# A new order around the two forms of seven products, second-weight sums on GpSimd, later stores of first weights

## The chip, the cores and the metric

The kernel runs on one core of one Trainium2 chip. The metric is the device time of one execution in microseconds (us); the median of three runs of the kernel before is 1193.54 us, from 1193.38 to 1194.54.

## The reference

Three stages in a row, on 2304 tokens of 512 features: attention over a small memory, a dense layer with a leaky activation, and four experts whose outputs are added with weights from normalized probabilities. The change touches the experts alone.

```python
def _moe2_ref(x, domain_probs, w1, w2):
    p = domain_probs / (domain_probs.sum(-1, keepdims=True) + 1e-09)
    out = np.zeros((N, D), dtype=np.float32)
    for e in range(E):                      # E = 4, D = 512, F = 1024
        h = np.maximum(x @ w1[e], 0.0)
        out += p[:, e:e + 1] * (h @ w2[e])
    return out.astype(np.float32)
```

## The kernel before

All products are made in a high and a low part: an operand is cast on ScalarE (the high part, `hi`) and the rest is subtracted on VectorE or GpSimd (the low part, `lo`), and three products of 128 x 288 stand for one (`PASSES`). What follows calls six or twelve such matmuls that stand together a block or a product.

The experts are done in *units*. A unit is 512 hidden features (`g`, 0 to 7) for 576 tokens (`b`, 0 to 3). The first half of the units (`half` 0) does b = 0 and 1 for all g, the second half b = 2 and 3; within a pair of units t = 0 and t = 1 stand for the two b. So there are 32 units, the first from 404 us on, the second half from about 790 us on.

Each unit makes the first product of the experts (class `Up`, twice: hp = 0 and 1) with seven block products p1 to p7 in place of eight. They are formed in three banks of PSUM, x, y and w: p1 and p2 into x; p6, p7 and p4 into y; p5 and p3 into w. Between them intermediate states are read: `v1` (ScalarE, of x after p1), `v16` (VectorE, y after p6, plus v1), `v167` (VectorE, y after p7, plus v1). p2 can start only when v1 has been read, p7 after v16, p4 after v167. `c11`, `c22`, `c21` and `c12` write the four blocks of the hidden layer, which is then gated (`gate`, `gate_half`: the maximum with 0 times the probability, on VectorE).

Between these blocks stand the *side products*, the second product of the experts for the unit before (`down()`, `old.product(n)`), each followed by a *flush* on VectorE or ScalarE that adds it to an accumulator. Their results take turns in two PSUM banks, so product n+2 waits for flush n. In most of the second half (`Seven`) the second product too has a form of seven, P1 to P7, two side products of six matmuls each (n = 0 to 13). Its operands are differences of blocks (`sum`, on VectorE, in place), cast (`hi`, ScalarE) and given a low part (`lo`, on GpSimd or VectorE). In the other units it has eight side products of twelve matmuls (`Down`). At the end `combine` adds the seven accumulators of b = 2 and 3 into four (seven sums each on VectorE).

The second weights have, for the form of seven, four sums S1, S2, S4, S3 (`s_sum`) whose parts (`s_part`) are made in the first half of the units and stored to memory; so are the parts of the first weights (`w1_lo`, `keep`, 1792 KB a store). Two S tiles and four part tiles are reused in turn, so a later cast waits for an earlier store.

There is no scheduler: each engine works its own queue in the order in which the code in `run_experts` issues. `extra(place)` issues what the table `more[(hp, place)]` holds: place 0 comes after v16, 1 after c11, 2 after c22, 3 after the gate, 4 after c12. Every transfer is issued on SyncE's queue (SP).

## Time and profile before

| | before |
|---|---|
| median of three runs | 1193.54 us |
| the profiled execution's own time | 1192.46 us |
| its span | 1190.7 us |
| TensorE busy (PE) | 1144.2 us, 96% |
| VectorE busy (DVE) | 871.6 us, 73% |
| ScalarE busy (ACT) | 472.8 us, 40% |
| GpSimd busy (POOL) | 378.3 us, 32% |
| experts, from the start | about 404 to 1188 us |

The profiled execution is one run beside the three; its span is what the trace covers. TensorE is nearly always busy, so its gaps are what to look for.

### The profile page before, as it was taken

How to read it: one execution, taken by the hardware profiler on the slowest of the kernel's cores; microseconds unless marked ns; L12 is line 12 of the kernel's file. 1: busy time of each engine (PE TensorE's matmuls, PEld its weight loads, DVE VectorE, ACT ScalarE, POOL GpSimd, SP SyncE). 2: the span in 40 equal slices, each digit the busy share in tenths (PEclk: the TensorE clock that was granted, in tenths of full speed). 3: DMA queues.
4: the chain of work that ended last, by engine and by line, in shares of the span. 5: the costliest groups of instructions: out<-in, count | busy, mean ns of one | idle time of the engine just before them, and what ended most of it. 6: DMA issues, size and time to landing. Idle time of an engine off the chain costs nothing.

```text
span 1190.7 us, 21752 instructions
## 1 busy us (share of the span) xinstructions
PE 1144.2 (96%) x8628; PEld 1093.4 (92%) x8628; DVE 871.6 (73%) x1601; ACT 472.8 (40%) x1035; POOL 378.3 (32%) x305
## 2 busy tenths in 40 slices
PE   8799999999999989999999999999999999999988
PEld 6578999999999989999999999899999999999988
DVE  6999888885567666666776676686577777777784
ACT  5567665554455534242232323233422222222220
POOL 2332023221010252554434535432323332333230
PEclk9999999999999999999999999999999999999999
DMA  9641221301000455464654554674555455545512
GB/s 377 258 173 28 63 90 53 107 20 79 1 1 1 179 199 222 169 228 187 221 211 175 195 228 178 208 269 163 179 173 164 151 170 150 164 151 187 158 48 71
DMA packets 64214, 180.02 MB, mean 151 GB/s; under 512 B 6640, under 2 KB 23024, under 8 KB 60400
## 3 DMA queue, kind: packets, MB, share of 16 engines
q1 hardware_dynamic: 64112, 178.63, 43.4%
q8 instruction: 68, 1.11, 0.4%
q14 instruction: 34, 0.28, 0.1%
HBM read 114.34 MB, written 64.26 MB: 150 GB/s over the span
## 4 chain that ended last, share of the span: by engine, by line
PE 71%; issue 13%; DVE 8%; POOL 4%; DMA 2%; ACT 2%; SPq 0%; DVEq 0%; ACTq 0%; POOLq 0%
PE o L908 16%; PE y L600 16%; PE h L562 8%; PE uy L802 8%; PE c L972 7%; PE ux L802 6%; PE uw L802 6%; POOL gc L232 3%; PE pw L523 2%; DMA kS<-S 1%; DVE S L232 1%; DMA rawin<-in_w_in 1%; DVE xt L664 1%; DVE g L232 1%; PE pm L325 0%
## 5 line engine op out<-in xcount | busy, mean ns | idle before, releaser
L908 PE MATMUL o<-g,w 128*128 128x288 f32 x1536 | 224.7, 295 | 0.9 <-DVE acc L925 0.9
L908 PEld LDWEIGHTS o<-g,w 128*128 128x128 f32 x1536 | 210.4, 188 | 1.6 <-DVE acc L925 1.3
L600 PE MATMUL y<-g,wout 128*128 128x288 f32 x1440 | 205.6, 297 | 0.0
L600 PEld LDWEIGHTS y<-g,wout 128*128 128x128 f32 x1440 | 194.2, 188 | 10.5 <-issue 7.0
L802 PE MATMUL uy<-x,w 128*128 128x288 f32 x1152 | 186.9, 297 | 13.9 <-DVE v L836 13.9
L802 PEld LDWEIGHTS uy<-x,w 128*128 128x128 f32 x1152 | 163.3, 189 | 18.4 <-DVE v L836 18.4
L972 PE MATMUL c<-gc,w2c 128*128 128x288 f32 x1008 | 164.3, 296 | 7.4 <-POOL gc L232 5.3
L972 PEld LDWEIGHTS c<-gc,w2c 128*128 128x128 f32 x1008 | 142.8, 188 | 10.9 <-POOL gc L232 8.5
L232 POOL TENSOR_TENSOR gc<-h,gc 128x576 fp32r<-128x576 f32 x56 | 88.3, 1597 | 169.2 <-issue 123.7
L802 PE MATMUL ux<-x,w 128*128 128x288 f32 x768 | 123.7, 296 | 5.6 <-ACT v L840 5.6
L232 POOL TENSOR_TENSOR w<-raww,w 128x512 fp32r<-128x512 f32 (+1 forms) x48 | 80.4, 1689 | 142.6 <-ACT w L507 82.4
L802 PE MATMUL uw<-x,w 128*128 128x288 f32 x768 | 122.5, 295 | 0.0
L802 PEld LDWEIGHTS ux<-x,w 128*128 128x128 f32 x768 | 109.3, 189 | 6.5 <-ACT v L840 6.5
L562 PE MATMUL h<-a,wp 128*128 128x288 f32 x720 | 108.8, 296 | 0.1
L802 PEld LDWEIGHTS uw<-x,w 128*128 128x128 f32 x768 | 108.8, 188 | 0.0
L925 DVE TENSOR_TENSOR acc<-o,acc 128x288 f32<-128x288 f32 x112 | 50.9, 454 | 75.0 <-PE o L908 75.0
L562 PEld LDWEIGHTS h<-a,wp 128*128 128x128 f32 x720 | 99.5, 188 | 2.7 <-issue 1.3
L581 DVE SCALAR_TENSOR_TENSOR pos<-neg,nal,pos 128x288 f32<-128x288 f32 x120 | 64.8, 545 | 43.0 <-ACT pos L576 42.5
L959 ACT CAST gc<-h 128x576 fp32r<-128x576 f32 x70 | 47.3, 676 | 119.0 <-DVE h L951 78.2
L836 DVE TENSOR_TENSOR v<-uy,v 128x288 f32<-128x288 f32 x128 | 58.0, 453 | 42.9 <-PE uy L802 41.9
L575 ACT ACTIVATE neg<-h 128x288 f32<-128x288 f32 x128 | 53.0, 414 | 83.7 <-PE h L562 78.6
L987 DVE TENSOR_TENSOR acc<-c,acc 128x288 f32<-128x288 f32 x96 | 43.6, 455 | 52.5 <-PE c L972 50.2
(163 smaller groups left out, 1624.3 us busy)
## 6 DMA issues: line engine op xcount, KB each, us to landing
kw<-w SPq DMA_DIRECT2D x16, 1792.0 KB, 7.1
raww<-in_w SPq DMA_DIRECT2D x32, 512.0 KB, 3.7
w<-kw SPq DMA_DIRECT2D x32, 512.0 KB, 4.7
kS<-S SPq DMA_DIRECT2D x56, 256.0 KB, 2.9
w2c<-kS SPq DMA_DIRECT2D x28, 512.0 KB, 3.6
kw<-w SPq DMA_DIRECT2D x25, 512.0 KB, 2.9
w<-kw SPq DMA_DIRECT2D x48, 256.0 KB, 4.4
kv<-in_kv SPq DMA_DIRECT2D x8, 1152.0 KB, 12.4
```

Of the source, the lines that this page charges most:

```text
L232: eng.tensor_tensor(out=out, in0=in0, in1=in1.bitcast(F32), op=ALU.subtract)
L562: mm(p, wp_t[b, c, f // 2][:, x, o2 + g * 256:o2 + g * 256 + 128], a_t[b][:, y, g, o:o + HB], start=(n == 0), stop=(n == 5))
L575: nc.scalar.activation(out=neg, in_=p, func=AF.Relu, scale=-1.0)
L581: nc.vector.scalar_tensor_tensor(out=pos, in0=neg, scalar=nal[:, ft:ft + 1], in1=pos, op0=ALU.mult, op1=ALU.add)
L600: mm(First.acc[d], w[:, x, d * 128:(d + 1) * 128], self.gt[:, y, 0:HB], start=(self.start and n == 0), stop=(self.stop and n == 2))
L802: mm(p, w[:, x, a, k], operand(self.b, i)[:, y, k], start=(start and n == 0), stop=(n == 5), skip_group_check=not start)
L836: nc.vector.tensor_tensor(out=out, in0=x, in1=y, op=ALU.add)
L908: mm(self.p, w[:, x, i, d % 2 * 128:(d % 2 + 1) * 128], g, start=(m == 0), stop=(m == 11))
L925: nc.vector.tensor_tensor(out=a, in0=self.p, in1=a, op=ALU.add)
L959: nc.scalar.copy(out=t[:, 0], in_=self.raw[q])
L972: mm(self.p, w[:, x, i, m * 128:(m + 1) * 128], self.g_t[q][:, y, i], start=(k == 0), stop=(k == 5))
L987: nc.vector.tensor_tensor(out=a, in0=self.p, in1=a, op=ALU.add)
```

## The change

Three edits. In `run_experts` the side products of the form of seven and the differences, casts and low parts of their operands are issued at other places: no side product between p5 and p2, two of them between p7 and p4; the differences of P7 and P6 of the unit before come earlier, that of P4 earlier and that of P5 later. The sums S1 to S4 move from VectorE to GpSimd, and the parts of S4 and S3 from the first unit of a pair into the second. The store of the first weights of hp = 1 is issued at the end of a pair's first unit, behind the stores of S1 and S2. With the last g, five of the seven `combine` sums of b = 2 are issued in the unit's second half and two in the next unit.

```diff
--- before.py
+++ after.py
@@ -709,6 +709,10 @@
             sub_to(eng, w[:, 1], src, w[:, 0])
         raw_t.pop(("w1", 2 * g + hp))
         load_raw()
+        if hp == 0:
+            w1_keep(g, hp)
+
+    def w1_keep(g, hp):
         kept_t["w1", g, hp] = keep(w1_t[g, hp], f"kw1{g}{hp}")
 
     def keep(t, name):
@@ -743,7 +747,7 @@
         t = pools["xt"].tile([128, 2, HB], F32, tag="xt", name=f"{n}{g}").rearrange("p k n -> p (k n)")[:, 0:512]
         cs_t[g, n] = [t]
         x, y = (cs_t[g, i][0] if i in ("S1", "S2") else a[i] for i in (x, y))
-        nc.vector.tensor_tensor(out=t, in0=x, in1=y, op=op)
+        nc.gpsimd.tensor_tensor(out=t, in0=x, in1=y, op=op)
 
     def s_part(g, n, part):
 
@@ -1024,13 +1028,19 @@
                     more.setdefault((1, 1), []).extend(f + (0,) for f in w2)
                 else:
                     more.setdefault((0, 0), []).extend(f + (1,) for f in w2)
+                if t == 0:
+                    more.setdefault((1, 4), []).append((w1_keep, g, 1))
                 if g < NG - 1:
                     for place, fs in (
                         ((1, 1), [(s_sum, g, "S1"), (s_part, g, "S1", 0)]),
                         ((1, 2), [(s_part, g, "S1", 1), (s_sum, g, "S2"), (s_part, g, "S2", 0)]),
-                        ((1, 3), [(s_sum, g, "S4"), (s_part, g, "S2", 1), (s_part, g, "S4", 0)]),
-                        ((1, 4), [(s_sum, g, "S3"), (s_part, g, "S4", 1), (s_part, g, "S3", 0)]),
-                    ) if t == 0 else (((0, 1), [(s_part, g, "S3", 1)]),):
+                        ((1, 3), [(s_part, g, "S2", 1), (s_sum, g, "S4")]),
+                        ((1, 4), [(s_sum, g, "S3")]),
+                    ) if t == 0 else (
+                        ((0, 1), [(s_part, g, "S4", 0)]),
+                        ((0, 2), [(s_part, g, "S4", 1), (s_part, g, "S3", 0)]),
+                        ((0, 4), [(s_part, g, "S3", 1)]),
+                    ):
                         more.setdefault(place, []).extend(fs)
 
             loads = {}
@@ -1042,8 +1052,11 @@
                 else:
                     loads = {2 * q + 1: [(w2_load, g, q % 2, q // 2)] for q in range(4)}
             if half and g == NG - 1:
-                for n in range(7):
-                    more.setdefault(((0, 2), (0, 3), (0, 4), (1, 0), (1, 2), (1, 3), (1, 4))[n], []).append((combine, b, n))
+                places = ((1, 2), (1, 3), (1, 3), (1, 4), (1, 4)) if t == 0 else ((0, 2), (0, 3), (0, 4), (1, 0), (1, 2), (1, 3), (1, 4))
+                if t == 1:
+                    more[0, 1] = [(combine, b - 1, 5), (combine, b - 1, 6)]
+                for n, place in enumerate(places):
+                    more.setdefault(place, []).append((combine, b, n))
             if n_unit > 1:
 
                 h0, g0, b0 = units[n_unit - 1]
@@ -1117,33 +1130,34 @@
                     last.lo(0, nc.vector if hp == 0 else nc.gpsimd)
                 extra(0)
                 down(hp == 1)
-                if hp == 1 and seven:
-                    c.sum(P5)
-                    c.hi(P5)
-                u.p5()
                 if old_seven:
-                    down()
-                    if hp == 1:
+                    if hp == 0:
+                        old.sum(P7)
+                        old.hi(P7)
+                        old.lo(P7, nc.gpsimd)
+                        old.lo(P3, nc.vector)
+                    else:
                         old.sum(P4)
                         old.hi(P4)
-                        old.lo(P6, nc.gpsimd)
+                u.p5()
                 u.p2()
                 u.c11()
                 down(hp == 1)
-                if old_seven and hp == 0:
-                    old.sum(P7)
-                    old.hi(P7)
-                    old.lo(P3, nc.vector)
                 extra(1)
                 u.p7()
                 u.v167()
                 u.c22()
+                extra(2)
+                down(True)
+                down()
+                if hp == 0 and old_seven:
+                    old.sum(P6)
+                    old.hi(P6)
+                if hp == 1 and seven:
+                    c.sum(P5)
+                    c.hi(P5)
                 if hp == 1 and old_seven:
                     old.lo(P4, nc.gpsimd)
-                extra(2)
-                down(True)
-                if hp == 1 and seven:
-                    c.lo(P5, nc.vector)
                 u.p4()
                 u.c21()
                 if seven:
@@ -1151,6 +1165,8 @@
                     if hp == 0:
                         c = Seven(g, b, u)
                         c.hi(P1)
+                        if old_seven:
+                            old.lo(P6, nc.gpsimd)
                         c.lo(P1, nc.gpsimd)
                     else:
                         c.second(u)
@@ -1159,14 +1175,14 @@
                 else:
                     u.gate(1)
                     if hp == 0:
+                        if old_seven:
+                            old.lo(P6, nc.gpsimd)
                         u.hi(1)
                         u.lo(1, nc.gpsimd)
                 extra(3)
                 down(True)
-                if hp == 0 and old_seven:
-                    old.sum(P6)
-                    old.hi(P6)
-                    old.lo(P7, nc.gpsimd)
+                if hp == 1 and seven:
+                    c.lo(P5, nc.vector)
                 u.p3()
                 u.c12()
                 extra(4)
```

How it moves instructions is seen at three places. The first is TensorE's queue in a unit of seven, here the one of g = 4 and b = 3 (it starts at 1003.1 us in the trace before), hp = 0. `uw430`, `ux430`, `uy430` are the banks w, x, y; `c420` to `c425` are the side products 0 to 5 of the unit before. Before:

```order
L802 MATMUL uy430_11879<-x31_9560,w170_8821 128x288 x6
L972 MATMUL c421_11892<-gc0_9598,w2c40_11642 128x288 x6
L802 MATMUL uw430_11900<-x31_9560,w170_8821 128x288 x6
L972 MATMUL c422_11907<-gc1_9751,w2c41_11675 128x288 x6
L802 MATMUL ux430_11864<-x33_9603,w170_8821 128x288 x6
L972 MATMUL c423_11923<-gc1_9751,w2c41_11675 128x288 x6
L802 MATMUL uy430_11879<-x33_9603,w170_8821 128x288 x6
L972 MATMUL c424_11945<-gc2_9867,w2c42_11715 128x288 x6
L802 MATMUL uy430_11879<-x35_9605,w170_8821 128x288 x6
L972 MATMUL c425_11965<-gc2_9867,w2c42_11715 128x288 x6
```

And with the change:

```order
L806 MATMUL uy430_11879<-x31_9560,w170_8821 128x288 x6
L976 MATMUL c421_11892<-gc0_9598,w2c40_11642 128x288 x6
L806 MATMUL uw430_11904<-x31_9560,w170_8821 128x288 x6
L806 MATMUL ux430_11864<-x33_9603,w170_8821 128x288 x6
L976 MATMUL c422_11919<-gc1_9750,w2c41_11688 128x288 x6
L806 MATMUL uy430_11879<-x33_9603,w170_8821 128x288 x6
L976 MATMUL c423_11938<-gc1_9750,w2c41_11688 128x288 x6
L976 MATMUL c424_11946<-gc2_9836,w2c42_11719 128x288 x6
L806 MATMUL uy430_11879<-x35_9605,w170_8821 128x288 x6
L976 MATMUL c425_11969<-gc2_9836,w2c42_11719 128x288 x6
```

The side product after p5 (`uw`) has gone behind p7 (the second row of `uy` with `x33`), so that two stand between p7 and p4 (`uy` with `x35`).

The second place is GpSimd's queue in the same unit: low parts of operands of the second product, from `h430` for P1 of this unit, from `h420` for P7, P6 and P4 of the unit before, from `c0` for P2; the last row belongs to the next unit. Before, in the order P1, P7, P6, P4, P2:

```order
L232 TENSOR_TENSOR gc0_9598<-h430_11921,gc0_9598 128x576
L232 TENSOR_TENSOR gc0_9598<-h420_11665,gc0_9598 128x576
L232 TENSOR_TENSOR gc1_9751<-h420_11665,gc1_9751 128x576
L232 TENSOR_TENSOR gc2_9867<-h420_11665,gc2_9867 128x576
L232 TENSOR_TENSOR gc2_9867<-c0_9699,gc2_9867 128x576
L232 TENSOR_TENSOR gc1_9751<-h520_12178,gc1_9751 128x576
```

And with the change, in the order P7 and P6 (one row), P1, P4, P2:

```order
L232 TENSOR_TENSOR gc0_9598<-h420_11661,gc0_9598 128x576 x2
L232 TENSOR_TENSOR gc1_9750<-h430_11917,gc1_9750 128x576
L232 TENSOR_TENSOR gc1_9750<-h420_11661,gc1_9750 128x576
L232 TENSOR_TENSOR gc2_9836<-c0_9697,gc2_9836 128x576
L232 TENSOR_TENSOR gc0_9598<-h430_11917,gc0_9598 128x576
```

P1 has moved behind P7 and P6, and P7 is the first of the unit, as the next unit's row shows too. The number of instructions is the same.

The third place is GpSimd's queue in the first pair of units (g = 0), from the gated block's low parts `g000` to those of the next unit's `g010`; `w2000` to `w2011` are low parts of the second weights. Before:

```order
L232 TENSOR_TENSOR g000_5173<-h000_5154,g000_5173 128x576 x2
L232 TENSOR_TENSOR w2000_5219<-raww20_3453,w2000_5219 128x512
L232 TENSOR_TENSOR w2010_5224<-raww21_5114,w2010_5224 128x512
L232 TENSOR_TENSOR w2001_5310<-raww20_3453,w2001_5310 128x512
L232 TENSOR_TENSOR w2011_5315<-raww21_5114,w2011_5315 128x512
L232 TENSOR_TENSOR g010_5372<-h010_5335,g010_5372 128x576
```

And with the change:

```order
L232 TENSOR_TENSOR g000_5171<-h000_5152,g000_5171 128x576 x2
L232 TENSOR_TENSOR w2000_5217<-raww20_3453,w2000_5217 128x512
L232 TENSOR_TENSOR w2010_5222<-raww21_5114,w2010_5222 128x512
L750 TENSOR_TENSOR S10_5227<-raww20_3453,raww21_5114 128x512
L750 TENSOR_TENSOR S20_5245<-S10_5227,raww20_3453 128x512
L750 TENSOR_TENSOR S40_5262<-raww21_5114,S20_5245 128x512
L750 TENSOR_TENSOR S30_5273<-raww20_3453 128x512
L232 TENSOR_TENSOR w2001_5299<-raww20_3453,w2001_5299 128x512
L232 TENSOR_TENSOR w2011_5304<-raww21_5114,w2011_5304 128x512
L232 TENSOR_TENSOR g010_5369<-h010_5324,g010_5369 128x576
```

The four sums `S10`, `S20`, `S40` and `S30` now stand between the two pairs of low parts; they were on VectorE.

## Rows read from the trace of the kernel before

**Rows 1.** The page's head: span, and busy time of each engine.

```profile
span 1190.7 us, 21752 instructions
PE 1144.2 (96%) x8628; PEld 1093.4 (92%) x8628; DVE 871.6 (73%) x1601; ACT 472.8 (40%) x1035; POOL 378.3 (32%) x305
```

**Rows 2.** Timeline of TensorE, 760 to 1150 us: start, length, instruction; brackets name waits.

```profile
828.92 0.93 PE L972 MATMUL c<-gc,w2c 128*128 128x288 f32 x5 [0.61 <-POOL gc L232]
852.18 0.92 PE L972 MATMUL c<-gc,w2c 128*128 128x288 f32 x5 [0.68 <-POOL gc L232]
869.69 1.06 PE L802 MATMUL uy<-x,w 128*128 128x288 f32 x6 [0.67 <-DVE v L836]
...
1018.09 0.93 PE L972 MATMUL c<-gc,w2c 128*128 128x288 f32 x5 [0.22 <-POOL gc L232]
...
1130.46 1.06 PE L802 MATMUL uy<-x,w 128*128 128x288 f32 x6 [0.67 <-DVE v L836]
```

**Rows 3.** Chain of waits, 905 to 1105 us: start, length, what.

```profile
909.96 10.37 issue
...
1099.64 10.37 issue
```

**Rows 4.** Timeline of one unit of seven, 1003 to 1029 us.

```profile
1004.73 0.96 PE L802 MATMUL uy<-x,w 128*128 128x288 f32 x6
1005.30 0.75 DVE L863 SCALAR_TENSOR_TENSOR c<-c,p 128x576 f32<-128x576 f32 x1
...
1009.49 0.96 PE L802 MATMUL uy<-x,w 128*128 128x288 f32 x6
...
1011.40 0.45 DVE L836 TENSOR_TENSOR v<-uy,v 128x288 f32<-128x288 f32 x1
...
1015.16 4.78 POOL L232 TENSOR_TENSOR gc<-h,gc 128x576 fp32r<-128x576 f32 x3 [10.39 <-issue]
...
1017.36 1.29 DVE L863 SCALAR_TENSOR_TENSOR h<-h,p 128x576 f32<-128x576 f32 x1
```

**Rows 5.** Timeline, 404 to 432 us, and a table by windows, whose header names its columns.

```profile
415.85 2.99 POOL L232 TENSOR_TENSOR w<-raww,w 128x512 fp32r<-128x512 f32 x2
...
418.84 0.95 PE L802 MATMUL uw<-x,w 128*128 128x288 f32 x6
...
423.65 0.62 ACT L755 CAST S<-S 128x512 fp32r<-128x512 f32 x1 [0.72 <-DMA kS<-S]
...
424.62 1.81 PE L802 MATMUL ux<-x,w 128*128 128x288 f32 x6 [4.82 <-ACT v L840]
...
429.32 0.96 PE L802 MATMUL uy<-x,w 128*128 128x288 f32 x6
...
core 0: us, PE busy (x) PEld busy (x) DVE busy (x) ACT busy (x) POOL busy (x), PEclk, DMA share, GB/s
...
424.60:429.00 4.40, 4.38 (x22) 4.38 (x23) 4.18 (x6) 2.45 (x5) 2.69 (x2) 0.64 0.76 249
```

**Rows 6.** Timeline of TensorE, 440 to 640 us: first and last of five waits.

```profile
474.54 1.06 PE L802 MATMUL ux<-x,w 128*128 128x288 f32 x6 [0.28 <-ACT v L840]
...
624.47 1.06 PE L802 MATMUL uy<-x,w 128*128 128x288 f32 x6 [0.67 <-DVE v L836]
```

**Rows 7.** Timeline of TensorE, 1122 to 1146 us.

```profile
1138.45 1.03 PE L972 MATMUL c<-gc,w2c 128*128 128x288 f32 x6 [2.15 <-DVE acc L987]
...
1143.60 0.93 PE L972 MATMUL c<-gc,w2c 128*128 128x288 f32 x5 [1.60 <-POOL gc L232]
```

**Rows 8.** Timeline of GpSimd (706 and 754 us) and of TensorE (712 us).

```profile
706.79 3.00 POOL L232 TENSOR_TENSOR w<-raww,w 128x512 fp32r<-128x512 f32 x2 [2.08 <-ACT w L507]
...
712.76 1.74 PE L908 MATMUL o<-g,w 128*128 128x288 f32 x12
...
754.46 2.55 POOL L232 TENSOR_TENSOR w<-raww,w 128x512 fp32r<-128x512 f32 x2 [2.08 <-ACT w L507]
```

## Prediction

> **What bounds the kernel now.** The page comes first: TensorE is busy for 1144.2 of 1190.7 us, VectorE for 73%, GpSimd for 32% [rows 1]. Time can be won only where TensorE stands still. The second view is therefore the timeline of TensorE alone; a bracket at a row's end names what it waited for. Of the waits between 404 us (start of the experts) and the end, the change touches three families.
>
> First, the units of seven products, from 813 us on. Twelve of them have a p4 that waits for VectorE's v167 (869.69 to 1130.46, one a unit), and each has a side product that waits for GpSimd's low half: 828.92, 852.18, then one a unit as at 1018.09 [rows 2]. Their cost is read from the chain of waits, where the same wait of GpSimd recurs every (1099.64 - 909.96) / 8 = 23.71 us, once a unit [rows 3]. A block of six matmuls takes (1009.49 - 1004.73) / 6 = 0.793 us where nothing waits [rows 4]; 28 of them are 22.2 us. So about 1.45 us a unit are lost, with a little left for the 28 starts. The two brackets say only 0.67 + 0.22 [rows 2]: a wait costs some 0.28 us more than its bracket.
>
> Second, the first half, where the sums of the second weights are made. One stall is large: p2 of the second unit stands for 4.82 us, because v1 is queued on ScalarE behind casts that wait for a store to land [rows 5]. From p5 (418.84) to p4 (429.32) lie p5, p2, p7 and a side product of two blocks, 5 x 0.793 = 3.97 us; the rows are 10.48 apart, so 6.5 us are lost. That is more than the wait: behind it TensorE's granted clock was 0.64 in the mean [rows 5], partly its level of 1.2 instead of 2.4 GHz. Five smaller waits lie between 474.54 and 624.47 (0.28, 0.65, 0.65, 0.52 and 0.67 us [rows 6]); with 0.28 each on top, 4.2 us.
>
> Third, the unit from 1122 to 1146 us: waits of 2.15 and 1.60 [rows 7].
>
> **The seven-product units.** The new order has two side products instead of one between p7 and p4, and one less between p5 and p2. v167 now ends at 1011.40 + 0.45 = 1011.85 where p4 was due at 1009.49 + 2 x 0.793 = 1011.08 [rows 4]. In the new order p7 is block 7 of the unit (from 0), ends at 8 x 0.793 = 6.35 us, v167 runs from 6.6 (TensorE's results are taken up 0.2 us after a block) to 7.05, and p4 is block 10, due at 7.9: margin 0.9. v16, which p7 needs, stays at about 3.2 against p7's 5.55.
>
> On GpSimd the low half of P7 stood second in a run of three of 1.6 each from 1015.16 [rows 4], and its product came before it was done. Now P7's sum is on VectorE at 3.8 to 4.4, its cast ends at 5.2, its low half at 6.7, and its product is block 17, due at 13.5. P6: sum 8.6 to 9.2, cast to 9.9, low half to 11.7, due at 22 x 0.793 = 17.4. P1 follows it to 13.2, due in the next unit. P4: sum from 14.9, low half to 17.9, due at 19.8. P5's slips to 22.5, due at 34 x 0.793 = 27. I can lay out no wait that is left. So 11 units give 1.45 each, 16.0; the first two, with a GpSimd wait alone, 0.61 + 0.28 and 0.68 + 0.28; the last one's p4, 0.67 + 0.28. Sum **18.7 us**.
>
> **The last units.** Five of the seven sums of b=2 go to the second half of the unit at 1122 us and two into the next. Both waits there go, 2.15 + 1.60 + 0.56 = 4.3. But at 22.3 us into that unit VectorE is behind: a gate, four sums of 0.7, three flushes and two adds after p4 keep it until about 25.2, the next gate to 25.9, v16 to 26.3, where p7 is due at 25.5; and the two sums push v167 0.7 us past p4. With restarts I give 1.9 back: **2.4 us** net, bounds 4.3 (no backlog) and 0.
>
> **The sums on GpSimd.** Seven pairs of units. The trace has no such sum on GpSimd; its nearest row is a low half of the same 128x512, two in 2.55 us alone and in 3.00 where VectorE works beside it [rows 8], so 1.28 to 1.5 each; I take 1.28. In the pair at 699 us the low halves begin at 706.79 and, with VectorE's sum gone, end at 709.3; S1 ends at 710.6, S2 at 711.9. ScalarE's cast of S1 (0.62) ends at 711.3. VectorE's low half of S1 waits for it, and behind that on VectorE stands the flush whose bank the product at 712.76 needs [rows 8].
>
> Does S2's sum hold this low half up as well? A gate on VectorE takes 0.75 us alone and 1.29 at 1017.36, inside GpSimd's run [rows 4]: an operation that reads two SBUF tiles waits for GpSimd's current one. Then the low half ends at 712.4, the flush at 712.8, and TensorE loses about 0.2 us in six of the pairs: **-1.2 us**. The Trainium skill speaks against the edit here, in "SBUF — State Buffer", section "Who interferes with whom": a VectorE instruction with two SBUF inputs and a GpSimd one that reads SBUF exclude each other, and the second fully blocks. By that rule the sum is the one below; were the engines independent, the flush would be done by 712.4 and the sum some 3 us better. The trace agrees (1.29 against 0.75).
>
> The gain there: the casts of S4 and S3 move into the next unit, when the stores of S1 and S2 have landed, and the 1.8 MB store of first weights no longer lies before those. The five small waits should go: **4.2 us**. The large one does not simply go. The first unit has no side products, so it is short. GpSimd's low halves begin at 415.85 [rows 5] and end at 418.2 to 418.4, S1 at 419.6, S2 at 420.9, and ScalarE reaches v1 only after S2's cast: 421.9, with p2 due at 419.64. VectorE is held by S1's low half until 421.4 and at two gates by S4's and S3's sums, so v16 ends near 425.8, and p7 starts there instead of at 426.22. With p4 at 428.4, if the clock does not fall behind these shorter waits, I count **0.8** of the 6.5; bounds 0 and 6.5.
>
> The later store costs nothing in my sum. Behind it on SP's queue stand the loads of the next raw weights, which GpSimd's w1 sums need 9 us later (at 724 us in that pair). Without that cover these sums slip by about 1 us, and no product waits for them at once.
>
> **Sum.** 18.7 + 2.4 - 1.2 + 4.2 + 0.8 = 24.9 us. The profiled execution took 1192.46 us (the span and 1.8 around it); that gives 1167.5. The median of the runs lies 1.1 above it, so **1168.5 us**.
>
> **Rivals.** (a) The sums on GpSimd cost more: the flush slips by one contended sum, 1.5 us instead of 0.2, in seven pairs: 25 - 7 x 1.3 = 16 us, 1177.5. For it: the flush has no margin, and ScalarE waits in order too. Against: GpSimd is busy for 32% of the span only [rows 1]. (b) The units of seven keep half of their loss, as a wait in another place (P4's low half, the densest one on GpSimd): 25 - 9 = 16, again 1177.5. Against: margins of 0.9 us and more. (c) The order brings nothing in those units, since the waits follow VectorE's total load and only move: 25 - 21 = 4, 1189.5. Against: the timeline names the same two places in every unit [rows 2]. (d) Slower: ScalarE's casts and VectorE queue behind the sums in the first half. That decides from 25 / 7 = 3.6 us lost in each pair, which two sums of 3 us instead of 1.28 would do; at 4.2 us a pair it ends near 1198. No GpSimd row of that size reaches 2 us. (e) Better: the first pair's 6.5 us go whole, no flush and no sum is late: 25 + 5.7 + 1.2 + 1.9 = 33.8, 1160.
>
> **How the numbers follow.** Forecast (1162 to 1174) 0.60, (a) 0.15, (b) 0.11, (c) 0.03, (d) 0.04, (e) 0.07. The likeliest is 1168.5. The range takes in (a) and (b) and stops short of (e): 1162 to 1180, leaving out (c), (d), (e) and tails. A difference under 0.2% (2.4 us) can't be told from none: faster 0.93, same 0.03, slower 0.04.
>
> **What would show it.** Right: the period of the units of seven falls from 23.71 to about 22.3 us, with no bracket on p4 or on P7's product; the five small waits of the first half are gone, and brackets of 0.1 to 0.2 us appear there on the last side product of a pair's first unit; p2 and p7 of the second unit still wait, with p4 near 428.5; in the last unit p7 and p4 wait for VectorE, 0.7 us each. Wrong: sums on GpSimd well over 1.3 us, casts of S1 or S2 that end after v1 was due, or TensorE waiting inside the units of seven.

## The result, and the profile after

The changed kernel takes 1174.71 us (median of four runs, 1174.5 to 1175.75), the kernel before, run beside it, 1193.9 us. The ratio is 0.984 (95% interval 0.982 to 0.986): faster, by 19 us. The prediction said 1168.5, with 1162 to 1180 as its range.

The page's head after, for [rows 1]:

```profile
span 1172.7 us, 21803 instructions
PE 1142.6 (97%) x8628; PEld 1096.0 (93%) x8628; DVE 844.3 (72%) x1573; ACT 473.0 (40%) x1035; POOL 406.7 (35%) x333
```

VectorE has 28 instructions fewer and GpSimd 28 more, the sums of seven groups. TensorE works almost as long as before; its waits have shrunk. What it waits for from the start of the experts, as total, times and longest:

```profile
PE uy L806 <- DVE v L840: 8.0, 7, 3.1
PE ux L806 <- ACT v L844: 2.2, 1, 2.2
PE o L912 <- ACT acc L927: 1.6, 1, 1.6
PE o L912 <- DVE g L232: 1.1, 2, 0.9
PE o L912 <- DVE acc L929: 0.8, 2, 0.6
PE c L976 <- ACT acc L989: 0.5, 2, 0.3
PE c L976 <- DVE acc3xt L991: 0.2, 1, 0.2
```

No line names GpSimd any more. The next view is TensorE's timeline, read by units: from a unit's first p1 to the next one's. In us, the profiled executions of before and after, and of three experiments told below:

| unit (half, g, t) | before | after | operands_moved | products_moved | sums_back |
|---|---|---|---|---|---|
| start of the experts | 404.48 | 406.18 | 404.58 | 404.37 | 405.01 |
| (0,0,1) | 30.33 | 31.90 | 31.05 | 30.69 | 27.31 |
| (0,1,0) | 24.12 | 25.71 | 24.11 | 24.12 | 24.13 |
| (0,1,1) | 25.30 | 23.83 | 25.31 | 25.31 | 23.83 |
| (0,2,0), as five of t = 0 | 23.83 | 24.10 | 23.83 | 23.83 | 23.84 |
| (0,3,1) | 24.95 | 23.83 | 24.58 | 24.56 | 23.84 |
| (0,4,1) | 25.55 | 23.84 | 25.47 | 25.56 | 23.83 |
| (1,0,1) | 23.18 | 22.79 | 22.31 | 23.13 | 22.79 |
| (1,1,0) | 23.25 | 22.82 | 22.31 | 23.21 | 22.82 |
| (1,2,0), as eleven of its kind | 23.71 | 22.28 | 22.31 | 22.92 | 22.28 |
| (1,7,0) | 27.47 | 22.67 | 24.39 | 26.42 | 22.67 |
| (1,7,1) to the end of the span | 41.54 | 42.96 | 41.47 | 41.53 | 43.24 |

The units of seven are the gain: 11 times 1.43 us. The other gain is (0,1,1), (0,3,1) and (0,4,1), 4.3 us together. Against that, (0,0,1) and (0,1,0) became longer by 1.6 us each. The experts' start 1.7 us later is no effect of the change, since nothing ahead of 404 us was touched, and the other kernels below start between 404.4 and 406.4 us. The last row is good to 0.05 us, since a page gives its span to 0.1.

One unit of seven after, TensorE's p1, p7, p4 and the next p1, and VectorE's v167, beside [rows 4]:

```profile
1017.95 0.95 PE L806 MATMUL ux<-x,w 128*128 128x288 f32 x6
...
1023.51 0.96 PE L806 MATMUL uy<-x,w 128*128 128x288 f32 x6
...
1024.50 0.46 DVE L840 TENSOR_TENSOR v<-uy,v 128x288 f32<-128x288 f32 x1 [0.34 <-PE uy L806]
...
1025.88 0.95 PE L806 MATMUL uy<-x,w 128*128 128x288 f32 x6
...
1040.23 0.95 PE L806 MATMUL ux<-x,w 128*128 128x288 f32 x6
```

v167 ends at 1024.96 and p4 starts at 1025.88 without a bracket: 0.9 us of lead, as laid out. VectorE itself waits 0.34 for p7, so no work is queued ahead of v167.

The first pair and the unit behind it, beside [rows 5]:

```profile
418.95 0.95 PE L806 MATMUL ux<-x,w 128*128 128x288 f32 x6
...
419.59 1.29 POOL L750 TENSOR_TENSOR S<-raww,raww 128x512 f32<-128x512 f32 x1
...
420.91 0.62 ACT L759 CAST S<-S 128x512 fp32r<-128x512 f32 x1 [3.53 <-POOL S L750]
...
421.56 1.21 DVE L232 TENSOR_TENSOR S<-S,S 128x512 fp32r<-128x512 f32 x1 [3.87 <-ACT S L759]
...
423.70 1.06 PE L806 MATMUL ux<-x,w 128*128 128x288 f32 x6 [2.21 <-ACT v L844]
...
425.54 1.26 POOL L750 TENSOR_TENSOR S<-raww 128x512 f32<-128x512 f32 x1 [1.36 <-DVE S L232]
425.80 1.62 DVE L884 SCALAR_TENSOR_TENSOR h<-h,p 128x576 f32<-128x576 f32 x1
427.34 0.44 DVE L840 TENSOR_TENSOR v<-uy,v 128x288 f32<-128x288 f32 x1
...
427.84 1.81 PE L806 MATMUL uy<-x,w 128*128 128x288 f32 x6 [3.08 <-DVE v L840]
429.45 3.08 PE L912 MATMUL o<-g,w 128*128 128x288 f32 x12
432.33 1.22 PE L806 MATMUL uy<-x,w 128*128 128x288 f32 x6
...
472.55 0.62 ACT L759 CAST S<-S 128x512 fp32r<-128x512 f32 x1 [3.37 <-POOL S L750]
...
474.43 0.69 ACT L927 COPY acc<-o 128x288 f32<-128x288 f32 x2
...
474.87 1.85 PE L912 MATMUL o<-g,w 128*128 128x288 f32 x12 [1.60 <-ACT acc L927]
```

ScalarE stands 3.53 us in front of the cast of S1, VectorE 3.87 us in front of its low part, and p2 and p7 wait for what is queued behind them. At 472 us the same stall lies ahead of a flush on ScalarE, and a side product waits 1.60. And behind the two waits the blocks are long: p7 has 1.81 instead of 0.96, the side product 3.08 instead of 1.74. The table by windows says why, in its column PEclk:

```profile
core 0: us, PE busy (x) PEld busy (x) DVE busy (x) ACT busy (x) POOL busy (x), PEclk, DMA share, GB/s
424.00:428.00 4.00, 0.92 (x7) 0.69 (x5) 3.97 (x6) 1.16 (x2) 1.44 (x2) 0.76 0.71 276
428.00:430.00 2.00, 2.00 (x9) 2.00 (x10) 1.44 (x3) 2.00 (x6) 1.22 (x1) 0.50 1.09 459
430.00:432.00 2.00, 2.00 (x10) 2.00 (x10) 1.97 (x3) 0.56 (x2) 1.50 (x2) 0.50 0.98 231
```

From 428 to 432 us TensorE ran at 1.2 instead of 2.4 GHz.

### The profile page after: what moved, and what is told of

Its sections match the earlier page's. It is cut to its first block, busy times and chain, and to the rows that moved or that the text cites. A ratio compares the mean times of both kernels' runs of the same rounds, so it can differ in the third digit from the quotient of the medians.

```text
span 1172.7 us, 21803 instructions
## 1 busy us (share of the span) xinstructions
PE 1142.6 (97%) x8628; PEld 1096.0 (93%) x8628; DVE 844.3 (72%) x1573; ACT 473.0 (40%) x1035; POOL 406.7 (35%) x333
## 4 chain that ended last, share of the span: by engine, by line
PE 87%; DVE 7%; DMA 2%; issue 1%; POOL 1%; ACT 1%; SPq 0%; DVEq 0%; ACTq 0%; POOLq 0%
PE o L912 18%; PE y L600 16%; PE c L976 13%; PE uy L806 12%; PE h L562 8%; PE ux L806 8%; PE uw L806 8%; PE pw L523 2%; DMA q<-in_q 1%; PE pc L357 1%; DMA w2c<-kS 1%; POOL g L232 0%; DVE h L884 0%; POOL w L232 0%; DVE xt L664 0%
## 5 line engine op out<-in xcount | busy, mean ns | idle before, releaser
L976 PE MATMUL c<-gc,w2c 128*128 128x288 f32 x1008 | 156.3, 295 | 0.5 <-ACT acc L989 0.5
L232 POOL TENSOR_TENSOR gc<-h,gc 128x576 fp32r<-128x576 f32 x56 | 82.9, 1489 | 145.4 <-ACT gc L963 98.5
L232 POOL TENSOR_TENSOR w<-raww,w 128x512 fp32r<-128x512 f32 (+1 forms) x48 | 76.6, 1611 | 98.4 <-ACT w L705 59.9
L844 ACT COPY v<-ux 128x288 f32<-128x288 f32 x64 | 25.6, 400 | 148.4 <-PE ux L806 142.2
```

Of the source, the lines that this page charges most:

```text
L232: eng.tensor_tensor(out=out, in0=in0, in1=in1.bitcast(F32), op=ALU.subtract)
L844: nc.scalar.copy(out=self.v1_t, in_=self.x)
L976: mm(self.p, w[:, x, i, m * 128:(m + 1) * 128], self.g_t[q][:, y, i], start=(k == 0), stop=(k == 5))
```

## Experiments

Every one is the kernel before with part of the change, or the changed kernel with part of it altered. Times are medians of four or five runs (`first_only`: eleven); the kernel before took 1193.3 to 1194.6 us beside them.

**The two halves of the change apart.** `seven_only` has the new order around the seven products and the moved `combine` sums; `first_only` has the rest (sums on GpSimd, later casts, later store). In `run_experts` and `s_sum`, against the changed kernel and against the kernel before:

```diff
-        nc.gpsimd.tensor_tensor(out=t, in0=x, in1=y, op=op)
+        nc.vector.tensor_tensor(out=t, in0=x, in1=y, op=op)
...
-                        ((1, 4), [(s_sum, g, "S3")]),
+                        ((1, 4), [(s_sum, g, "S3"), (s_part, g, "S4", 1), (s_part, g, "S3", 0)]),
```

```diff
-        nc.vector.tensor_tensor(out=t, in0=x, in1=y, op=op)
+        nc.gpsimd.tensor_tensor(out=t, in0=x, in1=y, op=op)
...
+                if t == 0:
+                    more.setdefault((1, 4), []).append((w1_keep, g, 1))
```

Expected of `seven_only`:

> The kernel before with the new order around the forms of seven and the moved combine sums alone; sums of the second weights on VectorE, their parts and the store of the first weights as before. My theory: this is the whole gain. By the units' starts in the two traces these stretches are worth 0.4 + 0.4 + 1.4 + 14.3 + 4.8 - 1.4 = 19.9 us, so about 1174.0 us, and the first half shows its old waits (4.8 us on p2 of the second unit, five small ones). Rival: the gain in the units of seven needs VectorE's relief in the first half or the later store, then well above 1178.

Measured: 1174.58 us, ratio 0.984 (0.983 to 0.986). Expected of `first_only`:

> The kernel before with the edits of the first half alone: sums S1 to S4 on GpSimd, parts of S4 and S3 in the second unit of a pair, later store. My theory: the old waits go (4.3 us) and new ones of the same size come (1.6 us in the second unit, 1.6 in the third, 0.27 in five pairs): 1193.9 + 0.2, between 1192.5 and 1195.5. As predicted before the change was run it would be 3.8 us faster, 1190. Rival: slower by more than 3 us, if the second unit's low clock weighs more without the rest.

Measured: 1193.1 us, ratio 1.000 (0.999 to 1.001). So the edits of the first half, 3.8 us of the predicted gain, are worth nothing as they stand; the whole gain comes from the edits of the second half.

**The sums alone, the store alone.** The changed kernel with one edit undone in each:

```diff
-        nc.gpsimd.tensor_tensor(out=t, in0=x, in1=y, op=op)
+        nc.vector.tensor_tensor(out=t, in0=x, in1=y, op=op)
```

```diff
-        if hp == 0:
-            w1_keep(g, hp)
+        w1_keep(g, hp)
...
-                if t == 0:
-                    more.setdefault((1, 4), []).append((w1_keep, g, 1))
```

> The changed kernel with the sums S1 to S4 on VectorE again, all else kept. My theory: the new waits of the first half come from the sums' place on GpSimd, through the casts of S1 and S2 that ScalarE waits for. So the 1.6 us in the third unit and 0.27 in five pairs go, and the second unit loses some 4 us less; the small old waits do not come back, since the parts stay moved: 1174.7 - 7 = 1167.5 us, from 1165 to 1170. Rival: VectorE, which gets four more operations a pair, shows the old waits of p4 again, 0.9 us in several pairs: 1172 or more.

Measured (`sums_back`): 1167.3 us, ratio 0.978 (0.977 to 0.979). Taking the sums to GpSimd costs 7.4 us; by the table it lies in (0,0,1), 4.6 us, (0,1,0), 1.6, and five units with 0.27 each. Some 1.5 of the 4.6 hang on the granted clock: three later kernels with the same waits as `sums_back` took 28.8 to 28.9 us for (0,0,1), not 27.31 (last section). So the sums' place costs 5.9 to 7.4 us.

> The changed kernel with the store of the first weights of hp = 1 back at its old place, all else kept. My theory: the old waits of ScalarE on landed stores were ended by moving the casts of S4 and S3, not by the store's place; 1174.7 within 1 us, with no new bracket in the first half. Rival: the early store (1.8 MB, 7 us) still lies in front of the stores of S1 and S2 or delays loads; then casts of S4 wait for DMA again and the second unit and some pairs lose 0.5 to 5 us: 1176 to 1180.

Measured (`early_store`): 1173.91 us, ratio 0.984 (0.982 to 0.985). The place of the store is worth nothing that can be measured.

**TensorE's order alone, the operands' places alone.** The prediction gave p4's half of the loss to TensorE's order and the other half to GpSimd's. Both from the kernel before:

```diff
                 if old_seven:
-                    down()
                     if hp == 1:
...
                 down(True)
+                down()
                 if hp == 1 and seven:
                     c.lo(P5, nc.vector)
                 u.p4()
```

```diff
                 down(hp == 1)
-                if hp == 1 and seven:
-                    c.sum(P5)
-                    c.hi(P5)
-                u.p5()
                 if old_seven:
-                    down()
-                    if hp == 1:
+                    if hp == 0:
+                        old.sum(P7)
+                        old.hi(P7)
+                        old.lo(P7, nc.gpsimd)
+                        old.lo(P3, nc.vector)
+                    else:
...
+                u.p5()
+                down()
```

> The kernel before with one edit: the two side products that stood between p5 and p2 stand between p7 and p4 instead (TensorE's order alone; the sums, casts and low parts of the seven operands keep their places, as do the sums of the second weights and the combining additions). Theory A, the prediction's: the wait of p4 for v167 (1.20 at 1009.49) is a lack of lead and goes in all twelve units of seven products with the half that runs after them, while the two waits for GpSimd's casts of P7 and the rest stay; about 12 x 0.95 = 11.4 us less, 1182. Rival B: the wait moves to p2, which now comes 1.6 us sooner behind p1 and waits for v1's copy or the bank; then 1188 to 1194. Rival C: the two side products that come later are the ones that then wait for P7's low part longer, or that no longer wait for it, since they are reached later; then the GpSimd waits shrink too and the time is nearer to 1176.

Measured (`products_moved`): 1183.45 us, ratio 0.992 (0.991 to 0.993). This is theory A, 1182. p4's waits (brackets of 0.67 [rows 2], not 1.20) are gone and the unit is 22.92 to 22.95 us; a product that waits for GpSimd stays, inside a block (1.34 instead of 0.96, here at 1012.73):

```profile
1010.23 4.77 POOL L232 TENSOR_TENSOR gc<-h,gc 128x576 fp32r<-128x576 f32 x3 [9.69 <-issue]
...
1012.73 1.34 PE L972 MATMUL c<-gc,w2c 128*128 128x288 f32 x6
```

> The kernel before with the new places of the sums, casts and low parts of the seven operands alone; TensorE's own order stays that of before, as do the sums of the second weights and the combining additions. Theory A: only the waits for GpSimd's low parts go, about 0.5 us in each of the twelve units, 6 to 7 us less, 1186 to 1187; p4 still waits for v167. Rival B: P7's sum and P3's low part leave VectorE's queue ahead of v167, so that v167 ends about 1.4 us sooner; p4's wait then goes as well without TensorE's order being touched, and the time is near 1176. Rival C: without the two side products behind p7 the sums that now stand ahead of p4 find their inputs late and hold c22 and c21: 1190 or more.

Measured (`operands_moved`): 1174.22 us, ratio 0.984 (0.982 to 0.985). Rival B holds: this one part gives as much as the whole change, and ends p4's wait as well, with one side product between p7 and p4 as before. The kernel before shows what stood in VectorE's queue just ahead of v167 (1011.40 in [rows 4], p7 from 1009.49):

```profile
1010.06 0.75 DVE L951 TENSOR_TENSOR h<-c,h 128x576 f32<-128x576 f32 x1
1010.73 0.75 DVE L232 TENSOR_TENSOR gc<-c,gc 128x576 fp32r<-128x576 f32 x1
```

In `operands_moved`, in the same half of a unit (it starts at 993.97), the place is empty and VectorE waits for p7:

```profile
1000.32 0.96 PE L802 MATMUL uy<-x,w 128*128 128x288 f32 x6
...
1001.32 0.46 DVE L836 TENSOR_TENSOR v<-uy,v 128x288 f32<-128x288 f32 x1 [0.34 <-PE uy L802]
...
1001.91 0.98 PE L802 MATMUL uy<-x,w 128*128 128x288 f32 x6
```

v167 ends at 1001.78 and p4 starts at 1001.91, 0.13 us later: enough. The third run on this is `old_products`, `sums_back` with TensorE's order of before:

```diff
                 u.p5()
+                if old_seven:
+                    down()
                 u.p2()
...
                 down(True)
-                down()
```

> The changed kernel with the sums of the second weights on VectorE (1167.3) and with TensorE's two side products back between p5 and p2; the sums, casts and low parts of the seven operands stay at their new places. Theory A, from the run with these places alone: the new places end both waits, TensorE's order adds nothing to them and costs 0.48 in each of the first two units of seven products, where its two flushes on ScalarE come one behind the other; the steady units are 0.03 longer. 1167.3 - 0.96 + 11 x 0.03 = 1166.7, and in the unit before the last 1.7 longer with the end 0.3 shorter or the same: 1166.7 to 1168.4. Rival B, the prediction's: the order of TensorE is what gives v167 its lead, and without it p4 waits 0.95 in each of twelve units, 1178.

Measured: 1168.01 us, ratio 0.978 (0.976 to 0.979). Theory A holds, though not its 1.7 us in (1,7,0), which took 22.32. TensorE's new order adds next to nothing to the operands' places (22.28 us a unit with it, 22.31 without); it costs about 0.5 us in (1,0,1) and (1,1,0), 22.31 without it and 22.8 with it.

**The combining additions.** `sums_back` with all seven of each part in their own unit, as before; and with those of b = 2 spread over the whole of (1,7,0):

```diff
-                places = ((1, 2), (1, 3), (1, 3), (1, 4), (1, 4)) if t == 0 else ((0, 2), (0, 3), (0, 4), (1, 0), (1, 2), (1, 3), (1, 4))
-                if t == 1:
-                    more[0, 1] = [(combine, b - 1, 5), (combine, b - 1, 6)]
-                for n, place in enumerate(places):
-                    more.setdefault(place, []).append((combine, b, n))
+                for n in range(7):
+                    more.setdefault(((0, 2), (0, 3), (0, 4), (1, 0), (1, 2), (1, 3), (1, 4))[n], []).append((combine, b, n))
```

```diff
-                places = ((1, 2), (1, 3), (1, 3), (1, 4), (1, 4)) if t == 0 else ((0, 2), (0, 3), (0, 4), (1, 0), (1, 2), (1, 3), (1, 4))
-                if t == 1:
-                    more[0, 1] = [(combine, b - 1, 5), (combine, b - 1, 6)]
+                places = ((0, 2), (0, 4), (1, 0), (1, 1), (1, 2), (1, 3), (1, 4)) if t == 0 else ((0, 2), (0, 3), (0, 4), (1, 0), (1, 2), (1, 3), (1, 4))
```

> The changed kernel with the sums of the second weights back on VectorE (1167.3 in its own run), and with the combining additions back in the places they had before, all seven of each part in its own unit from the third place on. By the prediction's two terms the waits of 2.15 and 1.60 ahead of the last unit come back and the 1.42 us by which the last unit had become longer are given back: 1167.3 + 3.75 - 1.42 = 1169.6. Rival: the unit before the last was long because of the old order of the seven products alone, and the additions were not what it waited for; then the time is 1165.9, faster than with the moved additions.

Measured (`combine_back`): 1168.67 us, ratio 0.979 (0.978 to 0.980). (1,7,0) takes 24.75 instead of 22.67, the last unit 41.58 instead of 43.24. The waits that come back are 1.01 and 0.55, not 2.15 and 1.60 [rows 7], so more than half of those two waits went with the other edits. By these units the move is worth 0.4 us. The profiled executions differ besides in (0,0,1), 28.84 against 27.31, of which more below.

> The changed kernel with the sums of the second weights back on VectorE (1167.3), and the seven combining additions of the third part spread over the whole of the unit before the last instead of five at its end and two at the start of the last. If the small waits in the last unit (0.6 and 0.4 us there in the changed kernel) are due to those two additions and to the five in front of them, they go: 1166.0 to 1166.5. Rival: the added lengths of the last unit come from VectorE's own tail (flushes with additions behind the last products), and the additions that now stand among the flushes of the seven products hold those instead: 1167.3 or more.

Measured (`best1`): 1166.82 us, ratio 0.977 (0.976 to 0.979), not told from `sums_back`. The waits of the last unit go (41.76), and a side product in (1,7,0) waits 0.91 for its flush in their place (23.46).

**Casts that come later, sums left on GpSimd.**

```diff
-                        ((1, 1), [(s_sum, g, "S1"), (s_part, g, "S1", 0)]),
-                        ((1, 2), [(s_part, g, "S1", 1), (s_sum, g, "S2"), (s_part, g, "S2", 0)]),
-                        ((1, 3), [(s_part, g, "S2", 1), (s_sum, g, "S4")]),
-                        ((1, 4), [(s_sum, g, "S3")]),
+                        ((1, 1), [(s_sum, g, "S1")]),
+                        ((1, 2), [(s_part, g, "S1", 0), (s_sum, g, "S2")]),
+                        ((1, 3), [(s_part, g, "S1", 1), (s_part, g, "S2", 0), (s_sum, g, "S4")]),
+                        ((1, 4), [(s_part, g, "S2", 1), (s_sum, g, "S3")]),
```

> The changed kernel with the casts and low parts of S1 and S2 each one place later, so that ScalarE and VectorE no longer come to them while GpSimd is still adding; the sums stay on GpSimd. Theory A: what the sums on GpSimd cost (7.4 us against the sums on VectorE) is mostly a stall in order, ScalarE standing 3.4 to 3.5 us in front of the cast of S1 with v1's copy or an accumulator's copy behind it, and VectorE 3.9 us in front of S1's low part; then the wait of 1.60 in the third unit goes, and the wait of 2.2 in the first pair shrinks by a us or more: 1174.7 - 1.6 - 1.0 to 2.5 = 1170.6 to 1172.1. Rival B: it is the slower gate (1.62 instead of 0.76 beside a GpSimd addition) and the later sums that count, wherever the casts stand: 1174.2 to 1175.2. The small 0.27 us in each later unit, which both leave open, are worth 1.4 in all: if they go too, theirs is the same stall.

Measured (`late_parts`): 1171.63 us, ratio 0.981 (0.980 to 0.982), as theory A said, though not in each place. Its waits in the first pair and the two units behind it, and ScalarE's cast of S1:

```profile
420.89 0.62 ACT L759 CAST S<-S 128x512 fp32r<-128x512 f32 x1 [4.05 <-POOL S L750]
...
423.20 1.06 PE L806 MATMUL ux<-x,w 128*128 128x288 f32 x6 [2.25 <-ACT v L844]
425.81 1.63 PE L806 MATMUL uy<-x,w 128*128 128x288 f32 x6 [1.55 <-DVE v L840]
...
470.79 1.85 PE L912 MATMUL o<-g,w 128*128 128x288 f32 x12 [0.26 <-ACT acc L927]
...
478.35 0.53 PE L912 MATMUL o<-g,w 128*128 128x288 f32 x2 [0.42 <-DVE g L232]
```

The 1.60 of the third unit fell to 0.26. In the first pair p7's wait fell from 3.08 to 1.55, while p2's, which was to shrink, stayed: one place later, ScalarE still came to S1 before the sum was done (4.05 us in front of the cast). The loss of 0.27 us left the units of t = 0 and came back as 0.2 in those of t = 1, and as 0.8 in (0,1,1) (24.62 instead of 23.83), behind the wait of 0.42 at 478.35. So 3.1 of the 7.4 us go when work on two other engines stands one place later; the rest stays with the sums on GpSimd.

**A version from all of it, and the two parts that count.** `best2` is `best1` with TensorE's old order, the additions earlier still, and in the first pair S4's and S3's sums behind v16:

```diff
+                if g == 0 and t == 0:
+                    for place in ((1, 3), (1, 4)):
+                        more[place] = [f for f in more[place] if f[0] is not s_sum]
+                if g == 0 and t == 1:
+                    more[0, 0] = [(s_sum, g, "S4"), (s_sum, g, "S3")] + more[0, 0]
...
+                places = ((0, 1), (0, 2), (0, 3), (0, 4), (1, 0), (1, 1), (1, 4)) if t == 0 else ((0, 2), (0, 3), (0, 4), (1, 0), (1, 2), (1, 3), (1, 4))
```

> Sums of the second weights on VectorE, the new places of the seven operands, TensorE's order of before, the third part's seven additions from the second place of the unit before the last on with the last one in its last place, and for the first group alone the sums S4 and S3 behind v16 instead of ahead of it. From the units of the other runs: 1166.8 with the additions spread; 0.9 less in the first two units of seven products, 0.3 more in the other ten; the wait of 2.36 for v16 in the first pair shorter by the two sums of 0.68 ahead of it, if nothing else is late then, 1.4 less; the 0.9 in front of the flush in the unit before the last gone. 1164.0. Rival: each of these only moves its wait on, to v167 in the first pair and to the tenth product in the unit before the last: 1166.5 to 1167.5.

Measured: 1170.6 us, ratio 0.980 (0.979 to 0.982), a miss. TensorE's waits, in the first pair and in (1,7,0):

```profile
421.32 1.06 PE L806 MATMUL ux<-x,w 128*128 128x288 f32 x6 [0.60 <-ACT v L844]
423.66 1.06 PE L806 MATMUL uy<-x,w 128*128 128x288 f32 x6 [1.28 <-DVE v L840]
428.73 1.06 PE L806 MATMUL uy<-x,w 128*128 128x288 f32 x6 [2.42 <-DVE v L840]
...
1115.90 1.05 PE L976 MATMUL c<-gc,w2c 128*128 128x288 f32 x6 [1.45 <-DVE acc L991]
1124.95 1.06 PE L806 MATMUL uy<-x,w 128*128 128x288 f32 x6 [1.24 <-DVE v L840]
```

v16's wait lost 1.1 us, and v167 took 2.42 in its place; the clock fell behind that. (0,0,1) took 30.47 us and (1,7,0) 26.12, against 27.33 and 23.46 in `best1`. VectorE's queue is full there, and a sum moved behind one reader stands ahead of the next.

`two_parts` is the kernel before with the operands' places, and with the later casts of S4 and S3; the sums stay on VectorE:

```diff
-                        ((1, 3), [(s_sum, g, "S4"), (s_part, g, "S2", 1), (s_part, g, "S4", 0)]),
-                        ((1, 4), [(s_sum, g, "S3"), (s_part, g, "S4", 1), (s_part, g, "S3", 0)]),
-                    ) if t == 0 else (((0, 1), [(s_part, g, "S3", 1)]),):
+                        ((1, 3), [(s_part, g, "S2", 1), (s_sum, g, "S4")]),
+                        ((1, 4), [(s_sum, g, "S3")]),
+                    ) if t == 0 else (
+                        ((0, 1), [(s_part, g, "S4", 0)]),
+                        ((0, 2), [(s_part, g, "S4", 1), (s_part, g, "S3", 0)]),
+                        ((0, 4), [(s_part, g, "S3", 1)]),
+                    ):
```

> The kernel before with two of the change's parts alone: the new places of the seven operands' sums, casts and low parts, and the later casts of S4 and S3 with their low parts. TensorE's order, the combining additions and the stores are those of before, and all sums of the second weights stay on VectorE. If these two parts hold all that the change gains, their gains add: the operands' places alone gave 1174.2, and the later casts with the sums on VectorE end the five small waits (4.3 us) and the large one of the first pair (1.5 to 3 us, as the granted clock goes there): 1174.2 - 5.8 to 7.3 = 1166.9 to 1168.4. Rival: TensorE's order or the moved additions are needed beside them, because VectorE's queue in the first units of seven products or in the unit before the last is fuller by the later casts: 1169.5 or more.

Measured: 1167.96 us, ratio 0.978 (0.977 to 0.980). The gains add. Of the change's six parts (TensorE's order, operands, sums, casts, store, additions) two, the operands and the casts, hold all of the gain within about 1 us of the best kernel tried (1166.82), and one, the sums, takes 6 to 7 us of it back.

## Why the prediction was right in kind and 6 us off

**The units of seven: right in size, wrong in cause for one part.** 1.45 us a unit were predicted and 1.43 measured, with no bracket left on p4 or on P7's product. But the step "the new order has two side products instead of one between p7 and p4" is not what was needed: `operands_moved` ends p4's wait without it. Either edit alone ends that wait; the prediction laid out the change only as a whole and did not look at what stood ahead of v167 on VectorE. The first two units gave 0.39 and 0.43 instead of 0.89 and 0.96: there the side products' flushes are copies on ScalarE, and of two side products in a row the second waits for one, in (1,0,1) at 828.71 and in (1,1,0) alike:

```profile
828.71 1.06 PE L976 MATMUL c<-gc,w2c 128*128 128x288 f32 x6 [0.26 <-ACT acc L989]
```

**The last units: right in size, by luck.** (1,7,0) and (1,7,1) gave 4.80 and took back 1.42, together 3.4; predicted were 0.95 for p4 and 2.4 for the moved additions. But `operands_moved`, with the additions at their old places, already has 3.1 of the 3.4 (24.39 and 41.47 against 27.47 and 41.54): the wait of 1.60 for GpSimd [rows 7] is gone there, and the one of 2.15 is shorter:

```profile
1119.08 1.06 PE L972 MATMUL c<-gc,w2c 128*128 128x288 f32 x6 [1.43 <-DVE acc L987]
```

So the step "both waits there go" by moving the additions was wrong: most of the gain belongs to the operands' places, and the move adds 0.2 to 0.4 us. What the move costs was right in kind; its two late waits stand where the text put them:

```profile
1133.63 1.06 PE L806 MATMUL uy<-x,w 128*128 128x288 f32 x6 [0.56 <-DVE v L840]
...
1136.67 1.07 PE L806 MATMUL uy<-x,w 128*128 128x288 f32 x6 [0.38 <-DVE v L840]
```

**The five small waits: right.** 4.2 predicted, 4.3 measured. With `sums_back` they go too, and in `seven_only` they stay, so the later casts with their stores end them, not the sums' engine; the store of the first weights has no part in it (`early_store`).

**The first pair: the step that failed.** p2 was put at 421.9 for a unit that started at 417.26, 4.6 us in; it came 4.75 us in (423.70 - 418.95). p7 was put 8.5 us in and came 8.9 in. The waits were right within 0.4. Then the proviso "if the clock does not fall behind these shorter waits" failed: p4 was due 11.1 us in and came 13.4 in (432.33), since p7 and the side product ran at half clock from 428 to 432 us. So the gain of 0.8 became a loss of 1.6. Behind waits of 2.2 and 3.1 us the clock fell to half in each of the three profiled executions that have them (the changed kernel, `first_only`, `early_store`).

**The sums on GpSimd: too cheap.** Their duration was right (1.28 assumed, 1.26 to 1.31 measured), though two readings of the trace before were not: GpSimd does have sums of 128x512 there, ahead of the experts (1.27 to 1.59 us), and three low parts of that size took 2.14 or 2.15. The wait was looked for in VectorE's flush, 0.2 us in six pairs; five have 0.27. In (0,1,0), where the accumulators are first written, the flush is ScalarE's, behind two casts that wait for GpSimd, and the unit lost 1.59. The prediction named ScalarE's order in rival (a) but counted it only in the first pair. The result lies between the forecast (up to 1174) and (a) (1177.5), and by mechanism it has a piece of each: the sums cost 7.4 us against the same kernel with them on VectorE, 4.6 of it (1.5 of that the clock's) in a pair that the sum had booked as a gain.

The gates there are long, 1.62 us at 425.80 beside the sum on GpSimd from 425.54, against 0.75 alone [rows 4]. The Trainium skill, "SBUF — State Buffer", section "Who interferes with whom", lets a VectorE instruction with two SBUF inputs and a GpSimd one that reads SBUF exclude each other; the trace agrees. How much of p7's 3.08 this makes was not separated from the stalls in order.

Worked out by the units, the span was put 6.9 us too short (24.9 us less predicted, 18.0 measured): 1.7 at the start, 2.4 in the first pair, 1.4 in (0,1,0), 0.3 in the five units, 1.0 in the first two of seven, 0.3 in the other eleven, less 0.1 in the five small waits, rounded.

## What to carry to other kernels

Where an order changes in two ways at once, ask of each wait what stands ahead of its releaser in that engine's queue: one edit may be enough, and the other one brings only its own price. Moving an operation to an idle engine is paid for in good part where its readers stand: two engines that work in order waited 3.5 and 3.9 us in front of operations of 0.6 to 1.2, with the critical copies behind them, and 3.1 of the 7.4 us went when these stood one place later. A wait of a few us that is cut in two need not get cheaper if TensorE's clock falls behind either.

## What was not expected of the hardware

The same waits do not always cost the same. `combine_back` and `best1` differ in the places of the `combine` sums alone, from 1099 us on, and have the same two waits in the first pair:

```profile
421.20 1.06 PE L806 MATMUL ux<-x,w 128*128 128x288 f32 x6 [0.59 <-ACT v L844]
424.62 1.58 PE L806 MATMUL uy<-x,w 128*128 128x288 f32 x6 [2.36 <-DVE v L840]
```

```profile
420.78 1.06 PE L806 MATMUL ux<-x,w 128*128 128x288 f32 x6 [0.60 <-ACT v L844]
424.20 1.06 PE L806 MATMUL uy<-x,w 128*128 128x288 f32 x6 [2.36 <-DVE v L840]
```

The granted clock from 424 to 428 us, in the same order (the sixth of the columns after the length):

```profile
424.00:428.00 4.00, 3.38 (x15) 3.39 (x16) 3.56 (x7) 3.05 (x6) 2.45 (x2) 0.61 1.18 455
```

```profile
424.00:428.00 4.00, 3.80 (x28) 3.80 (x29) 3.37 (x7) 3.30 (x7) 2.86 (x2) 1.00 1.08 414
```

The unit took 28.84 us in the one and 27.33 in the other, so the clock's fall alone is worth 1.5 us. It fell in three of the five profiled executions with these waits (`combine_back`, `old_products`, `two_parts`) and not in the other two (`sums_back`, `best1`). What decides it stays open. Differences of a us between such kernels can't be read from their medians, only from their units.
